# Batch 0's queries and keys loaded as 128 contiguous rows, and turned two tensors at a time into two banks

## Chip, cores and metric

One of the cores of a Trainium2 chip (trn2) runs the kernel; the other cores are idle. The metric is device time in microseconds (us) from the first to the last instruction of an execution, the median of several executions. The profile is of one execution of its own.

The engines: PE is TensorE's matmul, PEld its weight load, ACT is ScalarE, DVE is VectorE, POOL is GpSimd, SP is SyncE. SP and POOL only issue transfers for most of this kernel; sixteen DMA engines carry them out.

## What is computed

A causal attention with a sliding window of 64 over 8 batches, 8 heads, 576 positions and heads of 64; then a feed-forward layer with SiLU over the 4608 tokens of width 512:

```python
# q, k, v: (8, 8, 576, 64) float32;  w_in: (512, 2048);  w_out: (2048, 512)
scores = scale * np.matmul(q, k.transpose(0, 1, 3, 2))        # scale = 1/8
rel = pos[:, None] - pos[None, :]
mask = (rel >= 0) & (rel < 64)
scores = np.where(mask, scores, -1000000000.0)
attn = softmax(scores)                                        # along the keys
x = np.matmul(attn, v) -> transposed to (4608, 512)
h = x @ w_in
out = (h * (1.0 / (1.0 + np.exp(-h)))) @ w_out                # (4608, 512) float32
```

## The kernel before

Scores need q and k with the head dimension on the partitions, so both are turned. Batch 0 is loaded by plain loads and turned by TensorE against an identity; for later batches the kernel uses other forms, which the change leaves alone. In `qt` and `kt` a "pair" `pj` of two heads stands on 128 partitions, one head on each half; the two heads of a pair are two apart:

```python
    def head(pj, hh):
        return 4 * (pj // 2) + 2 * hh + pj % 2

    def pair(b, pj, kk):
        return (q, k)[kk][b, head(pj, 0):head(pj, 1) + 1:2]

    def load_cast(w, b, pj, kk):
        if b == 0:
            nc.gpsimd.dma_start(out=natbs[w][:, 0:S], in_=pair(b, pj, kk).rearrange("h (p m) d -> h p (m d)", m=NM0))
            return
        ...

    def load_first(i, kk):
        nc.sync.dma_start(out=nats[i][:, 0:2 * S].bitcast(FP32), in_=pair(0, 0, kk).rearrange("h (p m) d -> h p (m d)", m=NM0))

    def cast_first(e, i, w):
        copies[e](out=natbs[w][:, 0:S], in_=nats[i][:, 0:2 * S].bitcast(FP32))
```

`NM0` is 9 and `S` is 576, so that each partition gets nine successive positions of one head, 576 numbers of 4 bytes (2,304 bytes). Pair 0's q and k are loaded by SyncE as float32 and cast by ScalarE or VectorE; the other three pairs are loaded and cast by GpSimd's transfers. Each tensor is then turned by 18 transposes of 64x64 into one PSUM bank, and one copy ("lift") brings the bank to `qt` or `kt`:

```python
    def turn_first(op, w):
        pst = at_bf16(op).rearrange("x (m p) -> x m p", m=NM0)
        for m in range(NM0):
            for hh in range(2):
                r = slice(64 * hh, 64 * hh + 64)
                nc.tensor.matmul(
                    pst[r, m], lhsT=natbs[w][r, 64 * m:64 * m + 64], rhs=ident[r, r],
                    is_transpose=True, start=(m == 0), stop=(m == NM0 - 1),
                )

    def lift(e, op, b, pj, kk):
        m = NM if b else NM0
        copies[e](
            out=place_one(b, pj, kk).rearrange("x (p m) -> x p m", m=m),
            in_=at_bf16(op).rearrange("x (m p) -> x p m", m=m),
        )
```

Attention of batch 0 is six units (two halves of the heads, three groups of positions): scores in two banks, six exps of each half on ScalarE, the product with v, reciprocal and normalisation on VectorE, and a "way back" through TensorE that turns the result into `bridge`, the feed-forward layer's input. The first layer (line 401) multiplies `w_in` with `bridge`, ScalarE applies SiLU, the second layer (line 410) multiplies with `w_out`:

```python
    def first_layer(bank, j, ft, c, lo, hi):
        nc.tensor.matmul(
            banks[bank["bank"][0]][:, lo:hi], lhsT=w_in_sb[:, c, ft * 128:(ft + 1) * 128],
            rhs=bridge[:, (j * TT + lo) // 64:(j * TT + hi) // 64, c], start=(c == 0), stop=(c == NDC - 1),
        )
```

GpSimd issues its loads in this order: pair 1's q and k, two pieces of v, pairs 2 and 3's q and k, the other two pieces of v, eight pieces of `w_in`, batch 1's q, k and v with `w_out` after them, and so on.

The order of the instructions on every engine is made ahead of time by a small list scheduler (`Plan`), which has estimated durations and runs through the program once; the engines then follow that order. While there is nothing to multiply ahead of the first layer, it puts in filler matmuls ("warm", line 635) that keep TensorE awake:

```python
    def warm(op):
        nc.tensor.matmul(banks[op["bank"][0]][:, 0:384], lhsT=ident, rhs=ident.unsqueeze(1).to_broadcast([128, 3, 128]),
                         start=True, stop=True)

    p.add_filler(60, "warm", {"PE": 0.17}, warm, [c_ident], gate=lambda: moe[0][0]["seen"] is None,
                 pool="all")
```

Of the kernel before, what the change touches and what calls it, by code (L numbers as in the profile page):

```python
# [8 lines left out]
FP32 = mybir.dt.float32  # L9
BF16 = mybir.dt.bfloat16  # L10
# [101 lines left out]
def kernel(ctx, tc, q, k, v, w_in, w_out, out):  # L112
    nc = tc.nc
    B, H, S, D = q.shape
    d_model, d_ff = w_in.shape
    assert (B, H, S, D) == (8, 8, 576, 64) and (d_model, d_ff) == (512, 2048)
    NP = H // 2
# [15 lines left out]
    NM0, NR0 = 9, 64  # L133
# [8 lines left out]
    ident = keep.tile([128, 128], BF16, name="ident")  # L142
# [7 lines left out]
    nats = [keep.tile([128, 2 * NM * 128], BF16, name=f"nat{i}") for i in range(NN)]  # L150
    natbs = [keep.tile([128, 2 * NM * D], BF16, name=f"natb{i}") for i in range(NNB)]
# [11 lines left out]
    banks = [psum.tile([128, 512], FP32, name=f"at{i}") for i in range(4)]  # L163
    banks += [psum.tile([128, 512], FP32, name=f"mp{i}") for i in range(4)]

    p = Plan(
        {"at": range(4), "pv": range(4, 6), "mp": range(4, 8), "all": range(8)},
        rank=dict(prime=-8, early=-10, one=-9, first=-9, dma=-1, ld0=-1, ld1=-1, st=-2, xo=-1.5, xk=-1.4, silu=-3, out=-2, pv=0, ot=0, s=1, moe=99, warm=200, turn=2,
                  norm=0, inverse=0, bridge=0, exp=1, mask=1, lift=2, shift=2, cast=4, late=5, clear=9),
        rank0=dict(turn=-6, cast=-6, lift=-5, shift=-4.5, exp=-4, mask=-4, inverse=-3.5, norm=-3, bridge=-3.2),  # L170
        ahead=dict(s=-5.5, exp=-4.6, pv=-5.5, inverse=-4.3, norm=-4.2, ot=-5.5, bridge=-4.25),
    )
# [31 lines left out]
    def clear_k(i):  # L204
        nc.vector.memset(kt[i][:, 0:64].bitcast(FP32), 0.0)

    c_ident = p.add("one", {"POOL": 1.3}, const_ident)
    c_vv = [p.add("one", {"DVE": 0.25}, lambda _, i=i: clear_vv(i)) for i in range(NV)]
    c_k = [p.add("one", {"DVE": 0.15}, lambda _, i=i: clear_k(i)) for i in range(NK)]
# [6 lines left out]
    def head(pj, hh):  # L216
        return 4 * (pj // 2) + 2 * hh + pj % 2

    def pair(b, pj, kk):
        return (q, k)[kk][b, head(pj, 0):head(pj, 1) + 1:2]  # L220

    def load_cast(w, b, pj, kk):

        if b == 0:
            nc.gpsimd.dma_start(out=natbs[w][:, 0:S], in_=pair(b, pj, kk).rearrange("h (p m) d -> h p (m d)", m=NM0))
            return
        nc.gpsimd.dma_start(  # L227
            out=natbs[w][0:NR].rearrange("p (h y) -> p h y", h=2),
            in_=pair(b, pj, kk).rearrange("h (p m) d -> p h (m d)", m=NM),
        )  # L230

    def load_first(i, kk):
        nc.sync.dma_start(out=nats[i][:, 0:2 * S].bitcast(FP32), in_=pair(0, 0, kk).rearrange("h (p m) d -> h p (m d)", m=NM0))

    def cast_first(e, i, w):
        copies[e](out=natbs[w][:, 0:S], in_=nats[i][:, 0:2 * S].bitcast(FP32))  # L236
# [5 lines left out]
    def load_rows(i, b, pj, kk, hh):  # L242
        nc.gpsimd.dma_start(  # L243
            out=rows(i)[:, pj % 2, :, 64 * hh:64 * hh + 64],
            in_=(q, k)[kk][b, head(pj, hh)].rearrange("(m p) d -> p m d", p=NR),
        )

    def turn_rows(i, out):
        nc.sync.dma_start_transpose(
            out=out.rearrange("x (m p) -> x m p", m=2 * NM), in_=rows(i).rearrange("p j m x -> p (j m x)"))  # L250

    def place(b, pj, kk):
        return kt[b % NK][:, 64 + pj * S:64 + (pj + 2) * S] if kk else qt[b % NK][:, pj * S:(pj + 2) * S]
# [18 lines left out]
        )  # L272


    def at_bf16(op):
        return banks[op["bank"][0]].bitcast(BF16)[:, 0:S]

    def turn_first(op, w):

        pst = at_bf16(op).rearrange("x (m p) -> x m p", m=NM0)  # L280
        for m in range(NM0):
            for hh in range(2):
                r = slice(64 * hh, 64 * hh + 64)
                nc.tensor.matmul(  # L284
                    pst[r, m], lhsT=natbs[w][r, 64 * m:64 * m + 64], rhs=ident[r, r],
                    is_transpose=True, start=(m == 0), stop=(m == NM0 - 1),
                )

    def turn_heads(op, w):

# [18 lines left out]
    def place_one(b, pj, kk):  # L309
        return kt[b % NK][:, 64 + pj * S:64 + (pj + 1) * S] if kk else qt[b % NK][:, pj * S:(pj + 1) * S]  # L310

    def lift_twos(e, op, b, pj, hh, r):
        copies[e](  # L313
            out=place_one(b, pj, 0)[64 * hh:64 * hh + 64].rearrange("x (p m) -> x p m", m=NM)[:, :, r::2],
            in_=at_bf16(op)[64 * r:64 * r + 64].rearrange("x (h m p) -> x h p m", h=2, m=NM // 2)[:, hh],
        )

    def lift(e, op, b, pj, kk):
        m = NM if b else NM0
        copies[e](  # L320
            out=place_one(b, pj, kk).rearrange("x (p m) -> x p m", m=m),
            in_=at_bf16(op).rearrange("x (m p) -> x p m", m=m),
        )

    def shift_v(b, hf, a, z):
# [99 lines left out]
    kq_done, v_done, s_last, pv_last = {}, {}, {}, {}  # L425
    nat_free, natb_free = {}, {}
# [16 lines left out]

    def add_batch_qk(b):
        pool = "at" if b else "all"
        slot, parts = {}, {0: [], 1: []}
        for pj in range(NP):
            kq_done[(b, pj)] = []
            busy = s_last.get((b - NK, pj), []) + ([c_k[b % NK]] if b < NK else [])
            for kk in range(2):  # L450
                if b >= (NXK if kk else NXQ):
                    if pj % 2 == 0:
                        slot[kk] = n_nat[0] % NN
                        n_nat[0] += 1
                    i = slot[kk]
                    parts[kk] += [p.add("dma", {"POOL": 0.72}, lambda _, i=i, pj=pj, kk=kk, hh=hh: load_rows(i, b, pj, kk, hh),
                                        [nat_free.get(i)], dma=0.76) for hh in range(2)]
                    if pj % 2 == 0:
                        continue
                    both = busy + s_last.get((b - NK, pj - 1), [])  # L460
                    done = [p.add("xk", {"SP": 1.4}, lambda _, i=i, pj=pj, kk=kk: turn_rows(i, place(b, pj - 1, kk)),
                                  parts[kk] + both, dma=2.4)]
                    nat_free[i] = done[0]
                    parts[kk] = []
                    for x in (pj - 1, pj):
                        kq_done[(b, x)] += done
                    continue
                w = n_nat[1] % NNB
                n_nat[1] += 1
                if (b, pj) == (0, 0):  # L470
                    i = n_nat[0] % NN
                    n_nat[0] += 1
                    ld = p.add("ld0", {"SP": 0.45 if kk else 1.2}, lambda _, i=i, kk=kk: load_first(i, kk), dma=1.15)
                    ca = [p.add("cast", {"ACT": 0.84, "DVE": 0.56}, lambda e, i=i, w=w: cast_first(e, i, w), [ld], b=b)]
                    nat_free[i] = ca[0]
                else:
                    ca = [p.add("dma" if b or pj > 1 else "early", {"POOL": 0.66}, lambda _, w=w, pj=pj, kk=kk: load_cast(w, b, pj, kk),
                                [natb_free.get(w)], dma=0.55 if b else 0.75)]
                twos = b > 1 and not kk
                tu = p.add("turn", {"PE": 0.27 if twos else 0.5}, None, ca + [c_ident], lat=0.1, pool=pool, b=b)  # L480
                tu["fn"] = lambda _, tu=tu, w=w, twos=twos: (turn_twos if twos else turn_heads if b else turn_first)(tu, w)
                li = []
                if twos:
                    for hh, r in [(0, 0), (0, 1), (1, 0), (1, 1)]:
                        li.append(p.add("lift", {"ACT": 0.48, "DVE": 0.48}, lambda e, tu=tu, pj=pj, hh=hh, r=r:
                                        lift_twos(e, tu, b, pj, hh, r), [tu] + busy + li, b=b))
                else:
                    li.append(p.add("lift", {"ACT": 0.64, "DVE": 0.75}, lambda e, tu=tu, pj=pj, kk=kk:
                                    lift(e, tu, b, pj, kk), [tu] + busy, b=b))
                tu["untils"][0] = li  # L490
                natb_free[w] = tu
                kq_done[(b, pj)] += li
            if b < NIV and pj % 2:
                add_v_loads(b, [pj - 1, pj], [c_vv[b]])

    def add_v_loads(b, parts, busy):
        v_landed.setdefault(b, []).extend(
            p.add("dma", {"POOL": 1.0}, lambda e, part=part: load_v(e, b, part), busy, dma=1.53) for part in parts)
# [83 lines left out]
    def add_tile(j):  # L582
# [45 lines left out]
        free_gt.update(uses)  # L628

    add_batch_qk(0)  # L630
    add_batch_v(0)


    def warm(op):
# [4 lines left out]
                 pool="all")  # L639
# [51 lines left out]
```

## Time and profile before

| | |
|---|---|
| time, median of 3 | 332.39 us (331.53 to 333.81) |
| span of the profiled execution | 328.3 us |
| PE busy | 304.9 us (93%) |
| ACT busy | 183.2 us (56%) |
| POOL busy | 119.3 us (36%) |
| DVE busy | 94.6 us (29%) |
| read from memory, written | 36.70 MB, 9.44 MB |
| mean granted clock of TensorE | 0.979 |

The two layers are most of it. In the page's list of the costliest groups, a line of the kernel, its engine, the tiles, the count, and then busy time with the mean of one, and the engine's idle time ahead of it:

```profile
L401 PE MATMUL mp<-bridge,w_in_sb 128*128 128x512 bf16 (+2 forms) x640 | 130.5, 357 | 5.4 <-DMA bridge<-ox 3.4
L410 PE MATMUL mp<-w_out_sb,g 128*128 128x512 bf16 (+2 forms) x608 | 132.4, 368 | 0.0
```

A busy time is the sum of what the engine's instructions took; matmuls overlap, so means say little of one matmul by itself. In the page's slices a digit is the busy share in tenths of a fortieth of the span (8.2 us). "PEclk" is the share of TensorE's clock that was granted in the slice. The chain is followed back from the last instruction to whatever released each step; a load in it is counted from its issue to its landing.

### The profile page before, as it was taken

The page shows a single profiled execution, that of the slowest core. Times are in us where ns is not written, and L with a number is a line of the kernel's source. Part 1 is how long each engine was busy: PE and PEld are TensorE (multiplying, and loading weights), DVE is VectorE, ACT ScalarE, POOL GpSimd, SP SyncE. Part 2 cuts the span into 40 slices and gives each one's busy share as a digit, 9 for nine tenths or more (in the row PEclk, how much of TensorE's full clock was granted, in tenths as well). Part 3 has the DMA queues.
Part 4 walks back from the last instruction along what each step waited for, and adds up shares of the span by engine and source line. Part 5 has one row for each costly group of instructions (what it writes and reads, how often), then busy time and mean ns, then how long its engine had stood idle before and what let it go on. Part 6 is the DMA issues. An engine that isn't in the chain of part 4 may idle for free.

```text
span 328.3 us, 6842 instructions
## 1 busy us (share of the span) xinstructions
PE 304.9 (93%) x2788; PEld 154.3 (47%) x2788; DVE 94.6 (29%) x259; ACT 183.2 (56%) x340; POOL 119.3 (36%) x159
## 2 busy tenths in 40 slices
PE   5429999999999999958999999999999999999995
PEld 2216876554545445523455445544544444444444
DVE  1007543743557305720375036501400000000000
ACT  1017878767855766458754775477356226415611
POOL 8137586696789576873364000000000000000000
PEclk9759999999999999999999999999999999999999
DMA  5959999999999999999999994310410020021012
GB/s 57 118 60 157 196 164 198 164 162 229 159 172 174 130 168 165 155 143 175 157 152 139 166 225 114 94 20 2 112 66 0 32 90 9 0 85 45 0 62 68
DMA packets 142947, 37.60 MB, mean 115 GB/s; under 512 B 127812, under 2 KB 138180, under 8 KB 142916
## 3 DMA queue, kind: packets, MB, share of 16 engines
q0 software_dynamic: 100704, 18.09, 77.2%
q1 hardware_dynamic: 42212, 19.08, 30.6%
q8 instruction: 22, 0.36, 0.5%
q14 instruction: 9, 0.07, 0.1%
HBM read 36.70 MB, written 9.44 MB: 141 GB/s over the span
## 4 chain that ended last, share of the span: by engine, by line
PE 86%; DMA 9%; ACT 2%; issue 1%; DVE 0%; SPq 0%; ACTq 0%; DVEq 0%
PE mp L401 38%; PE mp L410 37%; DMA nat<-in_k_dram 6%; DMA bridge<-ox 3%; PE at L345 3%; PE mp L368 2%; ACT g L407 2%; PE at L368 1%; PE at L295 1%; PE at L304 1%; PE mp L284 1%; PE mp L635 1%; PE at L385 0%; PE at L635 0%; PE mp L385 0%
## 5 line engine op out<-in xcount | busy, mean ns | idle before, releaser
L401 PE MATMUL mp<-bridge,w_in_sb 128*128 128x512 bf16 (+2 forms) x640 | 130.5, 357 | 5.4 <-DMA bridge<-ox 3.4
L410 PE MATMUL mp<-w_out_sb,g 128*128 128x512 bf16 (+2 forms) x608 | 132.4, 368 | 0.0
L407 ACT ACTIVATE g<-mp 128x512 bf16<-128x512 f32 (+2 forms) x160 | 87.5, 555 | 35.7 <-PE mp L401 34.0
L401 PEld LDWEIGHTS <-w_in_sb 128*128 128x128 bf16 x640 | 60.7, 97 | 69.8 <-issue 12.0
L410 PEld LDWEIGHTS <-g 128*128 128x128 bf16 x608 | 55.8, 98 | 58.9
L416 ACT COPY ot<-mp 128x512 f32<-128x512 f32 (+2 forms) x32 | 17.8, 559 | 62.6 <-PE mp L410 47.2
L359 ACT ACTIVATE e<-at 128x384 bf16<-128x384 f32 x90 | 37.9, 497 | 17.7 <-PE at L345 15.4
L362 DVE TENSOR_TENSOR e<-e,mask 128x384 bf16<-128x384 bf16 x84 | 27.1, 354 | 49.9 <-ACT e L359 49.3
L243 POOL DMA_DIRECT2D nat<-in_k_dram x48 | 35.3, 741 | 16.3 <-DMA nat<-in_k_dram 5.6
L257 POOL DMA_DIRECT2D vv<-in_v_dram x32 | 31.9, 1007 | 20.0 <-DMA natb<-in_q_dram 9.8
L243 POOL DMA_DIRECT2D nat<-in_q_dram x32 | 24.5, 772 | 9.8 <-DMA vv<-in_v_dram 4.8
L381 DVE TENSOR_TENSOR ox<-mp,rc 128x384 bf16<-128x384 f32 x37 | 18.4, 539 | 0.1
L368 PEld LDWEIGHTS <-e 128*64 128x64 bf16 x576 | 11.5, 110 | 10.5 <-issue 8.3
L375 DVE RECIPROCAL rc<-mp 128x6 f32<-128x6 f32 x37 | 7.0, 194 | 22.7 <-PE mp L368 22.7
L345 PE MATMUL at<-qt,kt 64*128 64x64 bf16 x540 | 13.5, 191 | 0.0
L345 PEld LDWEIGHTS <-kt 64*128 64x128 bf16 x576 | 10.1, 95 | 6.5 <-issue 6.0
L330 DVE COPY vv<-vv 64x576 bf16<-64x576 bf16 (+1 forms) x14 | 8.1, 576 | 16.0 <-DMA vv<-in_v_dram 11.0
L236 ACT CAST natb<-nat 128x576 bf16<-128x576 f32 x2 | 1.3, 671 | 19.5 <-DMA nat<-in_q_dram 10.6
L635 PE MATMUL at<-ident 128*128 128x384 bf16 x22 | 7.6, 460 | 3.6 <-POOL ident L179 3.6
L313 DVE COPY qt<-at 64x288 bf16<-64x288 bf16 x17 | 8.1, 478 | 9.4 <-ACT qt L313 6.8
L368 PE MATMUL mp<-vv,e 128*64 128x65 bf16 x444 | 10.7, 196 | 0.0
L227 POOL DMA_DIRECT2D natb<-in_q_dram x12 | 7.9, 654 | 6.5 <-PE mp L401 3.0
(60 smaller groups left out, 142.6 us busy)
## 6 DMA issues: line engine op xcount, KB each, us to landing
out_dram<-ot SPq DMA_DIRECT2D x35, 256.0 KB, 4.0
vv<-in_v_dram POOLq DMA_DIRECT2D x32, 144.0 KB, 8.2
nat<-in_k_dram POOLq DMA_DIRECT2D x48, 72.0 KB, 7.5
nat<-in_q_dram POOLq DMA_DIRECT2D x32, 72.0 KB, 8.2
natb<-in_q_dram POOLq DMA_DIRECT2D x15, 144.0 KB, 7.7
w_in_sb<-in_moe_w_in_dram POOLq DMA_DIRECT2D x8, 256.0 KB, 8.3
w_out_sb<-in_moe_w_out_dram POOLq DMA_DIRECT2D x8, 256.0 KB, 8.2
natb<-in_k_dram POOLq DMA_DIRECT2D x7, 144.0 KB, 10.3
```

The source lines that it names most:

```text
L243: nc.gpsimd.dma_start(out=rows(i)[:, pj % 2, :, 64 * hh:64 * hh + 64], in_=(q, k)[kk][b, head(pj, hh)].rearrange("(m p) d -> p m d", p=NR),)
L257: queue[e].dma_start(out=vv[b % NV][:, 2 * g0 + 1:2 * g1 + 1:2, 0:D], in_=v[b].rearrange("h s d -> (h s) d").rearrange("(g p) d -> p g d", ...
L345: nc.tensor.matmul(at_six(of[hh])[:, j, x], lhsT=kt[b % NK][r, at:at + 128], rhs=qt[b % NK][r, at:at + 64], start=(b > 0 and j == x == 0), ...
L359: nc.scalar.activation(out=es[n % NE], in_=at_six(bank), func=ACTF.Exp, scale=scale)
L362: nc.vector.tensor_mul(es[n % NE], es[n % NE], mask0 if g == 0 else mask)
L368: nc.tensor.matmul(at_pv(bank)[64 * hh:64 * hh + 64, j, x], lhsT=es[(2 * n + hh) % NE][:, j, x], rhs=vv[b % NV][:, head(2 * a + j, hh) * N ...
L381: nc.vector.tensor_mul(ox(n), at_pv(bank)[:, :, :, 0:D], rcs[n % NRC].unsqueeze(3).to_broadcast([128, 2, 3, D]))
L401: nc.tensor.matmul(banks[bank["bank"][0]][:, lo:hi], lhsT=w_in_sb[:, c, ft * 128:(ft + 1) * 128], rhs=bridge[:, (j * TT + lo) // 64:(j * T ...
L407: nc.scalar.activation(out=gts[gt][:, lo:hi], in_=banks[bank["bank"][0]][:, lo:hi], func=ACTF.Silu)
L410: nc.tensor.matmul(banks[bank["bank"][0]][:, 0:hi - lo], lhsT=gts[gt][:, m * 128:(m + 1) * 128], rhs=w_out_sb[:, f, lo:hi], start=(f == 0) ...
L416: copies[e](out=ots[ot][:, lo:hi], in_=banks[bank["bank"][0]][:, 0:hi - lo])
L635: nc.tensor.matmul(banks[op["bank"][0]][:, 0:384], lhsT=ident, rhs=ident.unsqueeze(1).to_broadcast([128, 3, 128]), start=True, stop=True)
```

## The change

Batch 0's q and k are no longer loaded by the pairs that the scores want (two heads that are two apart), but by neighbouring heads `2u` and `2u + 1`. These two lie behind each other in memory, so that the source is one block of 128 rows of 576 numbers. A loaded tensor `u` therefore holds one half of each of two pairs. The turn takes two such tensors and puts the first halves of both into one bank and the second halves into another, so that each bank again holds a pair, as it did before. Its purpose is to let the loads be described as 128 contiguous rows. Data, copies and places in `qt` and `kt` are the same; the later batches' loads and turns are untouched.

```diff
+    def two(u, kk):
+        return (q, k)[kk][0, 2 * u:2 * u + 2].rearrange("h s d -> (h s) d").rearrange("(p m) d -> p (m d)", m=NM0)
+
     def load_cast(w, b, pj, kk):
         if b == 0:
-            nc.gpsimd.dma_start(out=natbs[w][:, 0:S], in_=pair(b, pj, kk).rearrange("h (p m) d -> h p (m d)", m=NM0))
+            nc.gpsimd.dma_start(out=natbs[w][:, 0:S], in_=two(pj, kk))
             return
...
     def load_first(i, kk):
-        nc.sync.dma_start(out=nats[i][:, 0:2 * S].bitcast(FP32), in_=pair(0, 0, kk).rearrange("h (p m) d -> h p (m d)", m=NM0))
+        nc.sync.dma_start(out=nats[i][:, 0:2 * S].bitcast(FP32), in_=two(0, kk))
...
-    def turn_first(op, w):
-
-        pst = at_bf16(op).rearrange("x (m p) -> x m p", m=NM0)
-        for m in range(NM0):
-            for hh in range(2):
-                r = slice(64 * hh, 64 * hh + 64)
-                nc.tensor.matmul(
-                    pst[r, m], lhsT=natbs[w][r, 64 * m:64 * m + 64], rhs=ident[r, r],
-                    is_transpose=True, start=(m == 0), stop=(m == NM0 - 1),
-                )
+    def turn_first(op, ws):
+
+        for u in range(2):
+            for m in range(NM0):
+                for j in range(2):
+                    r = slice(64 * j, 64 * j + 64)
+                    nc.tensor.matmul(
+                        banks[op["bank"][j]].bitcast(BF16)[64 * u:64 * u + 64, 64 * m:64 * m + 64],
+                        lhsT=natbs[ws[u]][r, 64 * m:64 * m + 64], rhs=ident[r, r],
+                        is_transpose=True, start=(m == 0), stop=(m == NM0 - 1),
+                    )
...
+                if b == 0:
+                    held[kk] = held.get(kk, []) + [(w, ca)]
+                    if pj % 2 == 0:
+                        continue
+                    ws, ca = [x[0] for x in held[kk]], [d for x in held.pop(kk) for d in x[1]]
+                    tu = p.add("turn", {"PE": 0.7}, lambda _, ws=ws: None, ca + [c_ident], lat=0.1, pool=pool, nb=2)
+                    tu["fn"] = lambda _, tu=tu, ws=ws: turn_first(tu, ws)
+                    for i in range(2):
+                        x = pj - 1 + i
+                        tu["untils"][i].append(p.add("lift", {"ACT": 0.64, "DVE": 0.75}, lambda e, tu=tu, x=x, kk=kk, i=i:
+                                                     lift(e, tu, 0, x, kk, i), [tu, c_k[0]]))
+                        kq_done[(b, x)] += tu["untils"][i]
+                    for x in ws:
+                        natb_free[x] = tu
+                    continue
```

The scheduler's durations of the loads are left as they were.

More of the change, by code (lines that the diff above doesn't have):

```diff
@@ L272, in load_w_out, with at_bf16 @@
         )
-    def at_bf16(op):
-        return banks[op["bank"][0]].bitcast(BF16)[:, 0:S]
-    def turn_first(op, w):
-        pst = at_bf16(op).rearrange("x (m p) -> x m p", m=NM0)
-        for m in range(NM0):
-            for hh in range(2):
-                r = slice(64 * hh, 64 * hh + 64)
-                nc.tensor.matmul(
-                    pst[r, m], lhsT=natbs[w][r, 64 * m:64 * m + 64], rhs=ident[r, r],
-                    is_transpose=True, start=(m == 0), stop=(m == NM0 - 1),
-                )
+    def at_bf16(op, i=0):
+        return banks[op["bank"][i]].bitcast(BF16)[:, 0:S]
+    def turn_first(op, ws):
[8 more added lines that the diff above has]
+                    )
     def turn_heads(op, w):
@@ L316, in lift_twos, with lift @@
         )
-    def lift(e, op, b, pj, kk):
+    def lift(e, op, b, pj, kk, i=0):
         m = NM if b else NM0
@@ L321, in lift @@
             out=place_one(b, pj, kk).rearrange("x (p m) -> x p m", m=m),
-            in_=at_bf16(op).rearrange("x (m p) -> x p m", m=m),
+            in_=at_bf16(op, i).rearrange("x (m p) -> x p m", m=m),
         )
@@ L445, in add_batch_qk @@
         pool = "at" if b else "all"
-        slot, parts = {}, {0: [], 1: []}
+        slot, parts, held = {}, {0: [], 1: []}, {}
         for pj in range(NP):
             kq_done[(b, pj)] = []
+        for pj in range(NP):
             busy = s_last.get((b - NK, pj), []) + ([c_k[b % NK]] if b < NK else [])
@@ L478, in add_batch_qk @@
                                 [natb_free.get(w)], dma=0.55 if b else 0.75)]
+                if b == 0:
[13 more added lines that the diff above has]
+                    continue
                 twos = b > 1 and not kk
                 tu = p.add("turn", {"PE": 0.27 if twos else 0.5}, None, ca + [c_ident], lat=0.1, pool=pool, b=b)
-                tu["fn"] = lambda _, tu=tu, w=w, twos=twos: (turn_twos if twos else turn_heads if b else turn_first)(tu, w)
+                tu["fn"] = lambda _, tu=tu, w=w, twos=twos: (turn_twos if twos else turn_heads)(tu, w)
                 li = []
```

## Prediction

> **What bounds the kernel now.** I read the page first: TensorE (PE) is busy 93% of 328.3 us, and the slices say where it is not.
>
> ```profile
> PE   5429999999999999958999999999999999999995
> PEclk9759999999999999999999999999999999999999
> DMA  5959999999999999999999994310410020021012
> ```
>
> Each digit is 8.2 us. PE is idle or half clocked only in the first three slices and in slices 18 and 19; everything else is a full PE. So time can be won at the start, or there. The chain that ended last, in order of time, names both:
>
> ```profile
> 0.74 0.71 SPq L233
> 1.51 20.70 DMA nat<-in_k_dram
> 22.23 0.68 ACT natb L236
> ...
> 134.08 10.01 DMA bridge<-ox
> ```
>
> One 288 KB load, batch 0's first k, is 20.7 us of the path. The waits within the first 40 us show who stands behind it and its sisters (total, times, longest):
>
> ```profile
> PEld L284 <- ACT natb L236: 11.9, 2, 8.2
> ACT natb L236 <- DMA nat<-in_q_dram: 10.6, 1, 10.6
> POOL vv L257 <- DMA natb<-in_q_dram: 9.8, 1, 9.8
> ACT natb L236 <- DMA nat<-in_k_dram: 8.9, 1, 8.9
> ```
>
> Why is that load slow? The transfers between 14 and 22 us:
>
> ```profile
> GB/s 139 139 145 145 139 139 116 122 105 117 117 111 128 92 110 87 82 60 60 64 75 63 63 46 46 46 46 46 46 46 46 46 69 46 46 64 106 135 142 152
> q1 hardware_dynamic: 111, 0.25, 8.7%
> ```
>
> Queue 1 carries only SyncE's loads here. Its 111 packets took 8.7% of 16 engines x 8 us = 11.1 us, 100 ns each (2,304 bytes), and 11.1/8 = 1.4 engines were at work on average. The floor of 46 GB/s is two such packets at a time: 2 x 2304 B / 100 ns = 46. The load runs on two engines of sixteen, beside other queues' packets. GpSimd's queue suffers as well:
>
> ```profile
> 8.68 0.82 POOL L225 DMA_DIRECT2D natb<-in_k_dram  x1
> 19.34 1.03 POOL L257 DMA_DIRECT2D vv<-in_v_dram  x1 [9.83 <-DMA natb<-in_q_dram]
> 22.68 1.01 POOL L257 DMA_DIRECT2D vv<-in_v_dram  x1 [2.32 <-DMA natb<-in_k_dram]
> 23.67 5.99 POOL L263 DMA_DIRECT2D w_in_sb<-in_moe_w_in_dram  x8
> ```
>
> GpSimd's loads take eight semaphores in turn in the built program, so the ninth (third v load) waits for the first (head pair 1's q) to land, and w_in starts 14.2 us after the queue stopped. The stages, with PE's busy time first and its clock after POOL:
>
> ```profile
> 3.60:10.10 6.50, 6.38 (x22) 2.94 (x22) 1.13 (x5) 0.00 (x0) 5.77 (x9) 1.00 1.01 98
> 10.10:22.90 12.80, 2.09 (x22) 0.99 (x22) 0.76 (x1) 1.34 (x2) 1.25 (x2) 0.59 0.72 97
> 22.90:26.10 3.20, 3.14 (x59) 2.25 (x60) 1.82 (x4) 1.28 (x3) 3.20 (x5) 0.50 1.08 63
> 26.10:36.10 10.00, 10.00 (x251) 6.49 (x250) 7.82 (x22) 8.19 (x17) 6.22 (x10) 1.00 1.37 176
> 36.10:328.30 292.20, 283.32 (x2437) 141.65 (x2435) 82.55 (x220) 171.14 (x318) 100.37 (x128) 1.00 1.10 115
> ```
>
> 22 fillers, then 12.8 us almost idle, 3.2 us of turns at half clock, 10 us of batch 0's attention, and from 36.1 the feed-forward with PE 97% busy.
>
> **What the Trainium skill says.** "DMA: Bandwidth & Descriptors", section "Why a DMA increments its semaphore by 16 and not by 1": a DMA runs on the largest k of at most 16 engines that divides the slowest dimension (not of size 1) of both access patterns. Before, the source is "h p (m d)", 2 x 64 x 576, against 128 partitions: k = 2. After, it is 128 x 576 on both sides: k = 16. The trace of before agrees with the two (46 GB/s). The same page, "Rules for kernel authors", advises 128 partitions outermost. "TensorE: Matmul & The Clock Gate", Part 1: the clock is halved after an idle window of about 3.4 us and given back after a busy one. The trace agrees: 0.50 between 14 and 23 us, and full again at 26.3, 3.4 us after the turns began.
>
> **The change part by part.** Same instructions in the same stages: 8 loads, 8 lifts of 128x576, and 4 turns of 36 transposes in place of 8 turns of 18. The built order shows the same GpSimd and SyncE sequences, 22 fillers ahead of the first turn as before, and only 7 fillers more in all.
>
> *Loads.* With k = 16, a load of 128 packets is 8 packets per engine: 8 x 100 ns = 0.8 us in place of 6.4 us on two engines alone. q is issued at 0.74 and k at 1.51; traffic in before begins at 2 to 3 us (transfers of the first 30 us), and I allow half a microsecond at the end, so my estimate is that q lands at 4 to 5 us, k at 5 to 6, and the two GpSimd loads (issued at 1.25 and 2.19) at 5 to 7. The casts (0.67 each) are done by 7.
>
> *The first turn then waits for the fillers.* They start at 3.64, go 0.32 us apart until about 9.05 and then at half that, and end at 10.03. That does not move. So the first turn starts at 10.0, on a warm clock, in place of 13.4 (q) and 22.96 (k).
>
> *From there to the feed-forward*, with durations from the timeline of before at full clock (18 transposes 0.36, score unit 0.70, value unit 0.38, filler 0.16, way back 0.25; DVE lift 0.76, ACT lift 0.64, exp 0.4, reciprocal 0.19, normalise 0.56, shift 0.35):
> - q's turn 36 x 0.02 = 0.72 to 10.8, three fillers to 11.3, k's turn to 12.0, six fillers to 13.0. The lifts of k end at 12.9.
> - Three score units to 15.1, first value unit to 15.5, fillers, second to 16.4.
> - Turns of head pairs 2 and 3 (16.5 to 18.0; their loads, issued 6.3 to 9.5, need to be down by 16.5 and should be by 13). DVE is the slower side: two normalisations to 17.25, then lifts of 0.76 each to 18.9.
> - Score units of the second half from 19.3 (after pieces of the way back, a value unit and fillers): 19.3, 20.0, 21.0. The six exps on ACT run 20.15 to 22.7; the value units follow at 21.7, 22.4 and 23.7.
> - First matmul of the first layer: 24.8, against 36.08 in before. **That is 11.3 us earlier.** The stretch from first score to first layer grows from 10.0 to 11.8, since the turns of pairs 2 and 3 now come together and later.
>
> *The loads behind.* The third v load goes out at 9.5 in place of 19.34, w_in at about 11.5 in place of 23.67: 12.2 earlier. In before the loads that wait for w_in by the eight semaphores go at 31.92, 33.20, 34.51, ..., so pieces land about 1.3 us apart, the eighth by 39.87. If the stream keeps its pace, the eighth lands at about 27.5, and the first layer wants it seven pairs of columns after 24.8, at about 30. The turns of batch 1 (42.2 to 48.6 in before, close upon their loads) come 11.3 earlier and their loads 12.2 earlier.
>
> *Sum.* After 36.1 nothing changes but bank numbers: a PE that is full for 283 of 292 us moves as a block. Gain 11.3 us. In the wait at 140.8 to 144.2 (3.4 us) PE waits for a transpose that stands in SyncE's queue behind transposes that wait for GpSimd's k and q loads; as those come 12.2 earlier and PE 11.3, up to 0.9 us more could go. I count 0.1. 332.4 - 11.4 = **321.0 us**.
>
> **Rivals.**
> 1. *w_in takes the place of k.* Before 36 us nothing waited for w_in, because it was behind the same delay. Loads of 8 x 288 KB, v and 4 MB of w_in now come in one unbroken stream; if q, k and v hold w_in up by 4 us more than I think, the first tile crawls at 1.3 us a piece against 0.67 us of PE work, and PE gets 7 to 8 us instead of 11: 325. For it: the queue share in 36 to 43 us is 1.66 already. Against: landing pace of 1.3 us and 2 to 3 us of slack by my count.
> 2. *The spread does not happen* (the two sides still split in two): then each turn waits for two tensors, the first q turn for pair 1's q too, at about 19 us, and the k turn for the later one as before: 332 to 333. Against: the program's source pattern is 128 long outermost, as for v and w_in, which do move at well over 46 GB/s.
> 3. *The middle takes it back.* The transpose wait at 134 to 144 could be set by transposes and stores of its own stretch (DMA share 2.0) and not move fully with the start: 2 to 3 us given back, 323 to 324. For it: 10.0 us for one transpose. Against: all that feeds it moves.
> 4. *More than this*: the clock's window falls early, the fillers end at 9 and the middle wait shrinks by 1: 319.
>
> **Range and chances.** The centre is 321.0. Runs of before span 331.5 to 333.8, so measuring alone is +-1. The start could be off by 1 us either way (fillers, half-clock window), rivals 1 and 3 pull up by 3 to 4, rival 4 down by 2. I take 317.5 to 325.0. Two per cent is 325.7: it takes rival 2, or 1 and 3 together, to miss it. Faster 0.91, same 0.07, slower 0.02.
>
> **What would show it.** Right: the chain has no 20 us load; the casts start before 8 us; the first turn (after the fillers) at about 10; no filler stretch at half clock at 23 to 26; w_in issued from 11 to 12 us; first first-layer matmul at 24 to 26; the middle wait still there, 2.5 to 3.5 us. Wrong: a wait of PE on w_in, or casts still waiting for their loads at over 10 us, or a stretch after the start that is longer than 292 us by more than 1 us.

## The result and the profile after

The changed kernel takes 320.72 us (median of 4 executions, 319.87 to 321.77) against 332.89 us beside it (331.53 to 333.81). The ratio is 0.964, with an interval of 0.959 to 0.969. A later comparison of the two gave 319.20 against 332.21, ratio 0.963 (0.959 to 0.967).

The page's slices of the changed kernel, each now 8.0 us:

```profile
PE   6999999999999999498999999999999999999996
PEclk9999999999999999689999999999999999999999
DMA  9999999999999999999999933301400110021012
```

The idle start is gone: the 2 and the 4 among PE's first digits are nines, the clock is full, and the DMA engines are busy from the first slice. But the weak spot in slice 17 is deeper than that of before (4 in place of 5), and the clock now falls with it, which it did not in the profiled execution of before.

The chain that ended last, in order of time (start, duration, what):

```profile
3.10 1.46 PE at L655 x4
...
8.94 0.59 PE mp L287 x34
9.53 0.59 PE at L655 x3
23.12 1.32 PE mp L405 x16
...
120.88 11.33 DMA bridge<-ox
132.35 11.13 PE mp L405 x40
```

No wait for a load stands at its start any more: after GpSimd's first two issues, which end at about 2.5 us and hold the making of the identity up, it runs through the fillers (line 655 in this kernel), and at 8.9 us goes on with the transposes (line 287). The 10.01 us for a transpose into `bridge` have become 11.33, and the 40 matmuls after it stand there with 11.13 us.

SyncE's two loads, in the transfers between 1 and 5 us, a column of 0.1 us each:

```profile
GB/s 0 0 0 0 0 0 0 138 184 161 92 115 69 23 161 323 346 461 369 369 461 369 415 415 392 369 369 288 277 231 219 219 184 150 196 184 173 184 207 196
nat<-in_q_dram SPq DMA_DIRECT2D x1, 288.0 KB, 2.9
nat<-in_k_dram SPq DMA_DIRECT2D x1, 288.0 KB, 3.2
```

Where 46 GB/s were the floor, 369 to 461 are now the plateau; k is landed 3.2 us after its issue, against 20.7. What that does to GpSimd's queue:

```profile
7.41 0.56 POOL L228 DMA_DIRECT2D natb<-in_k_dram  x1
7.93 2.04 POOL L260 DMA_DIRECT2D vv<-in_v_dram  x2
9.93 6.15 POOL L266 DMA_DIRECT2D w_in_sb<-in_moe_w_in_dram  x8
```

No wait stands between these; `w_in` goes out at 9.93 us, 13.7 us earlier. Of the four waits in the prediction's list, three are gone and ScalarE's for q is left with 1.6 us. That wait, and the one of batch 0's first lift:

```profile
ACT natb L239 <- DMA nat<-in_q_dram: 1.6, 1, 1.6
DVE qt L324 <- PE mp L287: 4.5, 1, 4.5
```

The second waits for the first turn, and so for the fillers ahead of that.

The first matmul of the first layer stands at 22.95 us against 36.08, 13.1 us earlier. The span is only 9.8 us shorter (318.5 against 328.3). The stages say where 3.3 us stayed. Before (PE's busy time first, the clock after POOL):

```profile
36.08:140.80 104.72, 104.34 (x1134) 57.11 (x1131) 50.21 (x126) 71.84 (x145) 79.87 (x103) 1.00 1.94 170
140.80:144.20 3.40, 0.00 (x0) 0.01 (x1) 1.21 (x4) 2.63 (x5) 2.14 (x3) 1.00 1.91 153
```

After:

```profile
22.95:127.60 104.65, 102.61 (x1118) 56.89 (x1128) 50.19 (x126) 71.40 (x144) 78.27 (x101) 1.00 1.94 169
127.60:132.30 4.70, 0.15 (x11) 0.03 (x2) 1.37 (x4) 2.80 (x5) 3.08 (x5) 0.78 1.86 155
132.30:146.00 13.70, 12.16 (x45) 4.95 (x46) 0.36 (x1) 8.71 (x13) 7.52 (x10) 0.83 1.71 154
```

From the first layer to the wait ahead of the fourth tile (the fourth 512 tokens of the feed-forward) both kernels need 104.7 us: the block moved whole. Then the wait is 4.6 in place of 3.4 us. And the first 40 matmuls of the fourth tile, in PE's order of time (start, busy, count, the wait ahead), of before and then of after:

```profile
144.22 8.79 PE L401 MATMUL mp<-bridge,w_in_sb 128*128 128x512 bf16 x40 [3.44 <-DMA bridge<-ox]
```

```profile
132.35 11.12 PE L405 MATMUL mp<-bridge,w_in_sb 128*128 128x512 bf16 x40 [4.60 <-DMA bridge<-ox]
```

2.3 us more for the same work on a clock of 0.83. So of 13.1 us, 1.2 went into a longer wait and 2.3 into the clock after it, and about 0.2 came back: 9.8 us between these two executions. The medians differ by more, 12.2 us: the profiled execution of before is itself 2.9 us below its median (330.02 against 332.89), that of after 0.5 below.

The clocks of the other executions bear on this. Of the 53 executions of before that ran beside the experiments, the 9 with a mean granted clock of 0.977 to 0.979 took 329.4 to 330.7 us, the 14 at 0.973 or 0.974 took 331.4 to 332.7, and 27 of the other 30, at 0.967 to 0.969, took 332.1 to 334.5. The profile of before, at 0.979, is of the first group. The half clock around the start of the changed kernel's fourth tile lasts from 130.3 to 137.1 us; 6.8 us at half clock are 0.010 of a mean clock over 328 us, and half of that is the step between two groups. So most executions of before seem to lose some 3.4 or 6.8 us more to half clock than the profiled one. Where, no trace of before shows. But the kernel with the new turns alone (below) is as slow as before and was profiled at 0.974, and there it is the middle:

```profile
145.20 10.34 PE L405 MATMUL mp<-bridge,w_in_sb 128*128 128x512 bf16 x40 [3.39 <-DMA bridge<-ox]
```

The 2.3 us are therefore a difference between two executions, and probably in good part not a cost of the change.

### The profile page after: what moved, and what is told of

It reads as the page before. It is cut to its first block, busy times and chain, and to the rows that moved or that the text cites. A ratio compares the mean times of both kernels' runs of the same rounds, so it can differ in the third digit from the quotient of the medians.

```text
span 318.5 us, 6825 instructions
## 1 busy us (share of the span) xinstructions
PE 302.4 (95%) x2766; PEld 153.6 (48%) x2795; DVE 95.9 (30%) x259; ACT 183.1 (57%) x340; POOL 118.4 (37%) x159
## 4 chain that ended last, share of the span: by engine, by line
PE 91%; DMA 4%; ACT 2%; issue 2%; POOL 0%; ACTq 0%; POOLq 0%
PE mp L405 40%; PE mp L414 37%; DMA bridge<-ox 4%; PE at L349 3%; PE mp L372 3%; PE at L655 2%; ACT g L411 2%; PE mp L655 2%; PE at L372 1%; PE at L299 1%; PE at L308 1%; PE at L389 1%; PE at L357 0%; PE mp L389 0%; PE at L287 0%
## 5 line engine op out<-in xcount | busy, mean ns | idle before, releaser
L405 PE MATMUL mp<-bridge,w_in_sb 128*128 128x512 bf16 (+2 forms) x640 | 132.8, 361 | 6.9 <-DMA bridge<-ox 4.6
L414 PE MATMUL mp<-w_out_sb,g 128*128 128x512 bf16 (+2 forms) x579 | 127.8, 367 | 2.6 <-issue 1.9
L246 POOL DMA_DIRECT2D nat<-in_k_dram x48 | 36.2, 760 | 15.1 <-DMA nat<-in_k_dram 6.9
L246 POOL DMA_DIRECT2D nat<-in_q_dram x32 | 24.1, 757 | 13.7 <-DMA nat<-in_q_dram 6.9
L385 DVE TENSOR_TENSOR ox<-mp,rc 128x384 bf16<-128x384 f32 x39 | 19.5, 540 | 0.2
L349 PE MATMUL at<-qt,kt 64*128 64x64 bf16 x546 | 13.1, 191 | 0.0
L372 PE MATMUL mp<-vv,e 128*64 128x65 bf16 x468 | 11.5, 197 | 0.0
```

The lines of the kernel that those rows point to most:

```text
L246: nc.gpsimd.dma_start(out=rows(i)[:, pj % 2, :, 64 * hh:64 * hh + 64], in_=(q, k)[kk][b, head(pj, hh)].rearrange("(m p) d -> p m d", p=NR),)
L349: nc.tensor.matmul(at_six(of[hh])[:, j, x], lhsT=kt[b % NK][r, at:at + 128], rhs=qt[b % NK][r, at:at + 64], start=(b > 0 and j == x == 0), ...
L372: nc.tensor.matmul(at_pv(bank)[64 * hh:64 * hh + 64, j, x], lhsT=es[(2 * n + hh) % NE][:, j, x], rhs=vv[b % NV][:, head(2 * a + j, hh) * N ...
L385: nc.vector.tensor_mul(ox(n), at_pv(bank)[:, :, :, 0:D], rcs[n % NRC].unsqueeze(3).to_broadcast([128, 2, 3, D]))
L405: nc.tensor.matmul(banks[bank["bank"][0]][:, lo:hi], lhsT=w_in_sb[:, c, ft * 128:(ft + 1) * 128], rhs=bridge[:, (j * TT + lo) // 64:(j * T ...
L414: nc.tensor.matmul(banks[bank["bank"][0]][:, 0:hi - lo], lhsT=gts[gt][:, m * 128:(m + 1) * 128], rhs=w_out_sb[:, f, lo:hi], start=(f == 0) ...
```

## Experiments

Theory A was that the spread of the loads over sixteen engines is the gain, and the turns into two banks only what allows it. Rivals were the turns (B), SyncE's loads alone (C) and GpSimd's queue alone (D). Four kernels take the change apart; each ran beside the kernel before, at 332.26 us (31 executions).

### The spread without the new turns

The kernel before, with each q and k load of batch 0 made as two loads of 64 rows:

```diff
-            nc.gpsimd.dma_start(out=natbs[w][:, 0:S], in_=pair(b, pj, kk).rearrange("h (p m) d -> h p (m d)", m=NM0))
+            for hh in range(2):
+                nc.gpsimd.dma_start(out=natbs[w][64 * hh:64 * hh + 64, 0:S],
+                                    in_=(q, k)[kk][0, head(pj, hh)].rearrange("(p m) d -> p (m d)", m=NM0))
...
-        nc.sync.dma_start(out=nats[i][:, 0:2 * S].bitcast(FP32), in_=pair(0, 0, kk)...)
+        for hh in range(2):
+            nc.sync.dma_start(out=nats[i][64 * hh:64 * hh + 64, 0:2 * S].bitcast(FP32),
+                              in_=(q, k)[kk][0, head(0, hh)].rearrange("(p m) d -> p (m d)", m=NM0))
```

> The turns of the kernel before (one tensor, one bank), but each of batch 0's q and k loads is made as two loads of 64 rows, one for each head, so that the slowest dimension is 64 on both sides. Theory A (the gain is the spread of the loads over sixteen engines, the turns are only what allows it): casts before 8 us, first turn at about 9 after the 22 fillers, first layer at 21.5 to 23.5, time 319 to 322. Rival B (the turns into two banks and their lifts bring part of it): first layer at 25 or later, 324 or more.

321.25 us, ratio 0.967 (0.961 to 0.973). ScalarE's order of time has the casts at 6.3 and 7.2 us:

```profile
6.29 0.67 ACT L240 CAST natb<-nat 128x576 bf16<-128x576 f32 x1
7.21 0.67 ACT L240 CAST natb<-nat 128x576 bf16<-128x576 f32 x1 [0.25 <-DMA nat<-in_k_dram]
```

First turn at 10.64 us (A had about 9) and first layer at 24.32, 1.4 later than in the changed kernel: twice as many issues put `w_in` at 12.94 in place of 9.93, and the identity (which GpSimd makes after its first loads) and with it the fillers start at 4.16 in place of 3.10. The intervals of the two kernels overlap. The time lies within A's range; the first layer comes 0.8 us later than A's range, and earlier than B's.

### The new turns without the spread

The changed kernel with the old form of the load. The halves then belong to other heads, so that scores of two heads in four are taken with each other's q and k; the amounts of work and of data are the same.

```diff
-        return (q, k)[kk][0, 2 * u:2 * u + 2].rearrange("h s d -> (h s) d").rearrange("(p m) d -> p (m d)", m=NM0)
+        return pair(0, u, kk).rearrange("h (p m) d -> h p (m d)", m=NM0)
```

> The changed kernel's turns and order, with batch 0's loads in the form of before (two heads that are two apart, 2 x 64 x 576; the output is then not the reference's, since the halves hold other heads). Theory A: first k lands at about 22 us as before, the turns now wait for two tensors each, first layer at 36 to 39, time 332 to 336. Rival B: below 328.

332.49 us, ratio 1.002 (0.998 to 1.005): no gain and no loss. First layer at 37.02 us. Its waits of the first 40 us show the old ones, and that the turn now waits for the second tensor too:

```profile
POOL vv L260 <- DMA natb<-in_q_dram: 9.8, 1, 9.8
ACT natb L239 <- DMA nat<-in_k_dram: 8.8, 1, 8.8
...
PEld L287 <- DMA natb<-in_q_dram: 5.2, 1, 5.2
```

A holds; B is out.

### SyncE's loads alone

> The kernel before, only SyncE's two loads (pair 0) are made of halves of 64 rows; GpSimd's six loads stay on two engines. Theory A with the eight semaphores as the second cause: pair 0 lands at 4 to 6 us, but pair 1's q and k are wanted for the first scores too and the third v load still waits for them; freed of SyncE's packets they land at 10 to 16 instead of 19 to 22. First layer at 26 to 31, time 322 to 328. If the queue of SyncE alone is the cause (rival C): 319 to 322, as in the changed kernel.

The second half of the first diff alone. 323.48 us, ratio 0.973 (0.968 to 0.979); first layer at 26.12 us. GpSimd's order of time:

```profile
8.69 0.82 POOL L225 DMA_DIRECT2D natb<-in_k_dram  x1
11.26 1.03 POOL L259 DMA_DIRECT2D vv<-in_v_dram  x1 [1.75 <-DMA natb<-in_q_dram]
12.76 1.01 POOL L259 DMA_DIRECT2D vv<-in_v_dram  x1 [0.48 <-DMA natb<-in_k_dram]
13.76 1.64 POOL L265 DMA_DIRECT2D w_in_sb<-in_moe_w_in_dram  x2
```

GpSimd's loads have their old form, but the wait of 9.83 us is 1.75. So three quarters of the gain (8.8 of 12 us) are had by two of eight loads. Time and first layer lie in A's ranges; the time is 1.5 us above C's.

### GpSimd's loads alone

> The kernel before, only GpSimd's six loads of batch 0 (pairs 1 to 3) are made of halves; SyncE's q and k stay on two engines, some 6.4 us each alone and more beside GpSimd's packets. Theory A: w_in is issued at 12 to 15 us, k lands at 16 to 20, first layer at 29 to 33, time 325 to 329. Rival C (SyncE's loads alone): no gain, 331 to 333. Rival D (GpSimd's semaphore wait is all of it): 319 to 322.

The first half of the diff alone. 331.00 us, ratio 0.995 (0.993 to 0.998). That misses D by far and A by 2 us, and `w_in` goes out at 22.18 us in place of my 12 to 15. It is what rival C said of this kernel, 331 to 333, although C had failed in the run above. GpSimd's order of time and the transfers from 8 to 20 us (0.3 us a column):

```profile
10.17 0.52 POOL L226 DMA_DIRECT2D natb<-in_q_dram  x1 [0.33 <-DMA natb<-in_k_dram]
18.43 0.52 POOL L226 DMA_DIRECT2D natb<-in_k_dram  x1 [7.74 <-DMA vv<-in_v_dram]
```

```profile
GB/s 86 94 150 170 197 211 200 167 175 141 179 164 136 149 72 55 49 41 41 49 33 48 41 40 49 41 41 49 33 48 49 32 48 30 20 20 26 23 42 88
```

The load that is waited for is v, and that one has 128 partitions outermost in every version. From about 12 us on only some 45 GB/s move, nearly all of it SyncE's q and k: between 12.2 and 18 us SyncE's queue moved 0.24 MB, and GpSimd's 0.03 MB in 121 packets. The reading that fits is that v's shares on SyncE's two engines stand among SyncE's packets, and that v counts as landed only with the last of them. The trace does not name the engine of a packet, so this is argued from the rates and from what waits for what, not shown. First layer at 33.30 us, 2.8 earlier than before; the time is only 1.3 less, and the wait ahead of the fourth tile is 4.60 here too, with half clock after it.

In the start of the first layer the parts nearly add: 10.0 us by SyncE's loads alone, 2.8 by GpSimd's alone, 11.8 by both in the same form, and 13.1 in the changed kernel. In the time they bring 8.8, 1.3, 11.0 and 12.2 us.

### The fillers ahead of the first turn, and the middle

The changed kernel ran again (319.20 us, 318.41 to 321.88), and beside it the first three kernels of this part; the last two ran together, later. All ratios are to the kernel before.

> The changed kernel once more, as the measure for the three kernels beside it: 320 to 322, ratio 0.96 to 0.97, a wait of 4 to 5 us ahead of the fourth tile of 512 tokens, and half clock after it.

The time is 0.8 us under my range, the ratio of 0.963 and the wait within theirs: the profiled execution has the first turn at 8.45, first layer at 22.97 and a wait of 4.17 us, and half clock follows (132.8 to 136.2 us).

**Eight fillers instead of 22**, by the gate of the fillers:

```diff
-    ... gate=lambda: moe[0][0]["seen"] is None,
+    ... gate=lambda: moe[0][0]["seen"] is None and (
+        p.queues["turn"][0]["seen"] is not None or sum(op["seen"] is not None for op in p.queues["warm"]) < 8),
```

> The changed kernel with 8 fillers instead of 22 ahead of the first turn. If the first turn waits for the fillers alone (the prediction's step): it starts at 5.3 to 6 us instead of 8.9, at half clock, and the first layer at 20.5 to 21.5 instead of 22.95. Theory M1 (the wait ahead of the fourth tile follows TensorE, since the transpose is issued when TensorE and VectorE are through): the gain goes through, 318 to 319.5. Theory M2 (the stream of loads sets that wait): the wait grows by what the start won, 320 to 321.5.

318.87 us, ratio 0.961 (0.957 to 0.964) against 0.963 (0.959 to 0.967): not to be told from the changed kernel. The first turn does start at 5.77 us, but at a slower pace, in PE's order of time:

```profile
5.77 0.99 PE L287 MATMUL at<-ident,natb 64*64 64x64 bf16 x36
```

and 0.66 us in the changed kernel. The granted clock reads 1.00 in both, as it does for the early fillers, which also go at half their later pace; so the trace does not call this half clock, though it looks like it. First layer at 21.65, 1.3 us earlier than 22.97 and just past my 20.5 to 21.5. The waits ahead of the fourth tile, of this kernel and of the changed one beside it:

```profile
130.91 10.48 PE L405 MATMUL mp<-bridge,w_in_sb 128*128 128x512 bf16 x40 [4.12 <-DMA bridge<-ox]
```

```profile
131.94 10.48 PE L405 MATMUL mp<-bridge,w_in_sb 128*128 128x512 bf16 x40 [4.17 <-DMA bridge<-ox]
```

The wait did not grow by what the start won. In the traces it follows PE, as M1 has it, and the span is 1.1 us shorter; in the times the difference is too small to be seen, so M1 rests on one trace of each kernel.

**Twenty fillers in the wait ahead of the fourth tile**:

```diff
     def first_layer(bank, j, ft, c, lo, hi):
+        if (j, ft, c) == (3, 0, 0):
+            for _ in range(20):
+                nc.tensor.matmul(banks[bank["bank"][0]][:, 0:384], lhsT=ident,
+                                 rhs=ident.unsqueeze(1).to_broadcast([128, 3, 128]), start=True, stop=True)
```

> The changed kernel with 20 fillers (128x384, some 3.3 us) put ahead of the fourth tile's first matmul, where TensorE waits 4.6 us for a transpose. Theory K (after that wait the clock is halved for some 3.4 to 6.8 us, and the first 40 matmuls take 11.1 us instead of 8.8): 1.5 to 2.5 us less than the changed kernel, and no half clock there. Rival: the clock costs nothing beside ScalarE's work: within 0.5 us of it.

317.63 us, ratio 0.958 (0.954 to 0.962), 1.6 us less than the changed kernel, as theory K has it, but with intervals that overlap at the edge. The trace shows the mechanism:

```profile
129.28 3.42 PE L407 MATMUL mp<-ident 128*128 128x384 bf16 x20
133.63 8.79 PE L409 MATMUL mp<-bridge,w_in_sb 128*128 128x512 bf16 x40 [0.93 <-DMA bridge<-ox]
```

The wait for the transpose is still there (3.42 of fillers and 0.93), but the clock stays whole, and the 40 matmuls take 8.79 us as in the profile of before. The span of this execution, one of the two longest of six, is no shorter than that of the changed kernel's (317.7 against 317.5): its first turn came at 9.66 us and its first layer at 24.55, 1.6 us later. From there to the end it needs 293.2 us against 294.5.

**Batch 3's way back by TensorE**:

```diff
-    NXQ, NXK, NXO = 4, 2, 3
+    NXQ, NXK, NXO = 4, 2, 4
```

> The changed kernel with batch 3's (and the last third of batch 2's) way back to the layer's input done by TensorE, as for batches 0 and 1, in place of transposes by DMA. It adds about 1.2 us of TensorE and 3.5 us of copies. Theory: the wait of 4.6 us ahead of the fourth tile goes, and with it the half clock: 314.5 to 317. Rival: the wait moves to the next tile, or the copies hold ScalarE up: 319 to 321.

In the code this moves the last third of batch 2 and the first two thirds of batch 3 to TensorE. 314.37 us, ratio 0.947 (0.943 to 0.950), a little better than I expected. Slices, and the fourth tile's start:

```profile
PE   6999999999999999999999999999999999999995
PEclk9999999999999999999999999999999999999999
```

```profile
128.83 1.26 PE L405 MATMUL mp<-bridge,w_in_sb 128*128 128x512 bf16 x5
```

The fourth tile starts 105.3 us after the first layer (23.53), without a wait ahead of it; the hole in the middle is gone, and does not come back at another tile. This beats both kernels.

**Both**, that is, eight fillers and batch 3 by TensorE, beside batch 3 by TensorE alone:

> Batch 3's way back by TensorE and 8 fillers instead of 22 ahead of the first turn, both on the changed kernel. With the wait ahead of the fourth tile gone, nothing in the middle can take back what the start wins: first layer at 21.5 to 22 us, and 1 to 1.7 us less than batch 3 by TensorE alone: 312.5 to 313.7. Rival: TensorE then runs into a wait on a load or transpose elsewhere, 314 to 315.

> Batch 3's way back by TensorE alone, once more, as the measure for the kernel beside it: 313.3 to 315.1.

313.25 us, ratio 0.942 (0.938 to 0.945), and 313.57, 0.943 (0.939 to 0.946). Both lie in their ranges, but the difference that I expected between them, 1 to 1.7 us, is 0.3 and not to be told from none. First layer at 20.91 and 22.87, 2.0 us apart, but spans of 311.0 and 311.5. PE in the kernel with both changes:

```profile
26.64 0.75 PE L405 MATMUL mp<-bridge,w_in_sb 128*128 128x192 bf16 x7 [0.28 <-DMA w_in_sb<-in_moe_w_in_dram]
...
28.91 0.45 PE L299 MATMUL at<-ident,natb 96*64 96x96 bf16 x12 [0.28 <-DMA natb<-in_q_dram]
```

Here rival 1 of the prediction begins: with a start 2 us earlier, PE waits for `w_in` and batch 1's q and k, which does not happen in the kernel beside it, whose PE has no wait in that stretch. Of its lead of 2.0 us, 0.8 are left when the next long row of first-layer matmuls starts (30.12 against 30.89 us). In this kernel the start has come up to its loads.

## Why the prediction was right

The time lies 0.3 us from the centre, but two steps were off in opposite directions. That they cancel so closely is luck; the direction and the greater part of the gain are not.

*Two engines to sixteen.* Right. The section "Why a DMA increments its semaphore by 16 and not by 1" of the Trainium skill's "DMA: Bandwidth & Descriptors" gives the number of engines, and the rates of both traces agree: 46 GB/s before, 369 to 461 after. The new turns alone gave 1.002, the spread alone 0.967.

*GpSimd's queue.* Right in kind: `w_in` at 9.93, predicted 11.5. What I had not counted is that an issue of such a load takes GpSimd 0.56 us in place of 0.82. What I had missed, and the GpSimd-only kernel showed, is how much of the queue's delay was SyncE's doing.

*The first turn waits for the fillers.* Right: casts from 3.67, first turn at 8.87. I said "that does not move" and 10.0; but the identity is made 0.54 us earlier, since GpSimd issues two loads ahead of it, and the 22 fillers were through in 5.8 us in place of 6.4. In later executions with 22 fillers the turn stood at 8.4 to 9.7 us, so this term is uncertain by a microsecond.

*From there to the feed-forward.* 14.1 us, predicted 14.8. With the earlier turn the first layer came at 22.95 in place of 24.8: the gain at the start was 13.1 us, not 11.3, and the prediction's 24 to 26 was missed on the early side.

*A PE that is full moves as a block.* Right to 0.1 us: 104.72 and 104.65 from the first layer to the middle wait.

*The middle.* This step failed. I wrote that "up to 0.9 us more could go", reasoning that the loads came earlier still than PE, and counted 0.1. The wait got longer, by 1.2 us. Every profiled kernel with an earlier first layer and the same way back has it at 3.9 to 4.6 us, the two with the old start at 3.4. A sign of being wrong that the prediction named came true with it: from the first layer to the end it is 295.6 us, more than 1 us over 292. Of rival 3's "2 to 3 us given back" the traces show 3.5: 1.2 by the wait and 2.3 by the clock, which I had not thought of, and which the median of before probably holds in part already. The transpose is issued when PE and VectorE are through, 13.2 us earlier like everything else, and it is its own stay in the DMA queues, 11.3 us against 10.0, that sets the wait; starting earlier does not shorten it. Why it stayed 1.3 us longer is open: between issue and landing the DMA share is 1.99 there and 2.05 before. Its issue alone takes 5.04 us on SyncE's queue, against 3.08, so part of the delay stands there already.

*The clock.* The rule of the Trainium skill's "TensorE: Matmul & The Clock Gate", Part 1, that I used for the start bears on the middle too, where I did not use it: an idle window of about 3.4 us halves the clock. The traces agree only roughly: 3.39 us was followed by half clock in the new turns alone and 3.44 was not in before, and in the changed kernel the clock fell 2.5 us after PE had stopped.

*Rivals 1 and 2.* Rival 1 does not occur in the changed kernel, but begins 2 us further on. Rival 2's 332 to 333 is what the new turns alone measured, 332.49.

By the two profiled executions the sum is: the start gained 1.8 us more than predicted, the middle gave back 3.5, and the medians differ by 2.4 us more than these executions do. If the median of before has the half clock of the middle too, the last two largely cancel, and what is left of the middle's cost is the longer wait.

## What to carry to other kernels

Look at the outermost dimension on both sides of every load: two heads on the outside cost a 288 KB load 20.7 us where 128 rows cost 3.2, and splitting it into loads of 64 rows brought nearly the same (321.25 against 320.72 us, with overlapping intervals). In this kernel a slow load was paid for by the loads beside it as well, so look first for the one that the others wait behind: SyncE's two loads brought three quarters of the gain, GpSimd's six alone almost nothing. When a start moves, go through the waits further on with the clock in mind: in these traces a wait of 3.4 us and more was in all but one followed by half clock, which cost 1.3 to 2.3 us beyond its length, and a few fillers in it, or taking its cause away, belong to the change. And look at the clocks of all executions before setting two profiles against each other: that of before was of its fastest group.

## What the runs showed that I had not expected

- The half clock around the fourth tile lasted either 3.4 or 6.8 us, and the wait ahead of it does not alone decide which, or whether it comes. By wait, with the time of the 40 matmuls (8.79 us on a full clock):

| kernel | wait, us | half clock, us | 40 matmuls, us |
|---|---|---|---|
| before | 3.44 | none | 8.79 |
| new turns alone | 3.39 | 3.4 | 10.34 |
| halves of 64 rows | 3.92 | 3.4 | 10.13 |
| eight fillers | 4.12 | 3.4 | 10.48 |
| changed, again | 4.17 | 3.4 | 10.48 |
| SyncE's loads alone | 4.20 | 3.4 | 10.48 |
| GpSimd's loads alone | 4.60 | 6.8 | 10.93 |
| changed | 4.60 | 6.8 | 11.12 |

- The issue of a GpSimd load of 128 rows takes 0.55 us, of the same bytes as 2 x 64 rows 0.81 us.
- A load on sixteen engines (v) kept GpSimd waiting for 7.74 us beside two loads on two engines, while some 45 GB/s moved.
